# Seven block products for eight in the last batch's out-projection of an attention and feed-forward kernel

## The chip, the cores and the metric

One core of one Trainium2 chip. The time is the device time of one execution in microseconds (us), as a median over runs. A profile's times count from its own first instruction, and its span is some 1.7 us shorter than the device time. Two kernels are called faster or slower than each other from 2% on; a smaller difference can still be clear of noise, and then its interval says so.

## The reference

```python
def sm_attn(qq, kk, vv):
    s = scale * np.matmul(qq, kk.transpose(0, 1, 3, 2))
    ...                                   # row softmax -> a
    return np.matmul(a, vv)
p_packed = sm_attn(p, k, v)               # 8 batches, 8 heads, 32 packed rows, head size 64
out = sm_attn(q, p_packed, p_packed)      # 576 rows a head
x = out.transpose(0, 2, 1, 3).reshape(4608, 512)
h = x @ w_in                              # 512 -> 2048
g = h * np.cos(h)
return (g @ w_out).astype(np.float32)     # 2048 -> 512: the out-projection
```

## The kernel before

The eight batches run as a pipeline. While TensorE computes the hidden layer of batch b (`h_mm`, sixteen column blocks of 128), the out-projection of batch b-1 is fed in between as filler, one matmul per `fill` step.

```python
def recips(b):                     # for the NEXT batch, on VectorE
    ...
    V.reciprocal(r1[b], sums1[b])
    V.tensor_scalar(out=rs1[b], in0=r1[b], scalar1=scale, scalar2=None, op0=ALU.mult)   # 128x2

def normalise(b):                  # a2n: what h_mm(b) multiplies
    ...
    for y in range(2):
        V.scalar_tensor_tensor(out=a2n[b][:, y], in0=a2u[b][:, y], scalar=r1[b][:, y:y + 1],
                               in1=lns[b][:, y], op0=ALU.mult, op1=ALU.mult)   # two inputs in SBUF

def h_mm(b, fc):
    ...                            # 4 matmuls -> PSUM, cosine on ScalarE
    def rest():
        V.tensor_tensor(out=gT[b][:, fc, :]..., in0=ps[:, :, 0:HS], in1=csv, op=ALU.mult)  # PSUM and SBUF
        if fc % 8 == 7:
            G.tensor_copy(out=joint[b // 2][...], in_=gT[b][...])                # GpSimd

for s in range(3, B):
    ...
    permute_v(s + 1)               # GpSimd copy of the next batch's v
    ...
    recips(s + 1)
    ...
    sums2(s, 0); fill(5); sums2(s, 1)
    normalise(s)
    ...
    fill(13)
    slot(s, [(5, ...pp(s + 1)...), (10, ...pw2(s + 1)...)], 5, {10: 3})   # h_mm(s, 0..15), hooks, filler
set_filler(B - 1); fill(1000)      # last batch: 4 chunks x 16 matmuls of 128x512
tail_chunk(B - 1, 4)               # joint chunk of batches 6 and 7: 32 matmuls of 128x256
```

The softmax here doesn't subtract the row's maximum and nothing guards it: scores larger than these inputs give would overflow.

Of the kernel before, what the change touches and what calls it, by code (L numbers as in the profile page):

```python
# [8 lines left out]
FP32 = mybir.dt.float32  # L9
BF16 = mybir.dt.bfloat16  # L10
AF = mybir.ActivationFunctionType
ALU = mybir.AluOpType
# [3 lines left out]
def kernel(  # L16
# [8 lines left out]
    out: bass.AP,  # L25
):
    nc = tc.nc
    B, H, S, D = q.shape
    NP = p.shape[2]
    DM, DF = moe_w_in.shape  # L30
    scale = 1.0 / (D ** 0.5)
    NFC = DF // 128
    C = 6
    TP = S // C
    HS = S // 2
    PSUM = bass.MemoryType.PSUM
    EXP_SET = "natural_log_exp_and_others"
    SIN_SET = "trig_and_small"
# [1 line left out]
    const = ctx.enter_context(tc.tile_pool(name="const", bufs=1))  # L40
    bf_pool = ctx.enter_context(tc.tile_pool(name="bf", bufs=1))
    vp_pool = ctx.enter_context(tc.tile_pool(name="vp", bufs=2))
    att_pool = ctx.enter_context(tc.tile_pool(name="att", bufs=1))
    a2n_pool = ctx.enter_context(tc.tile_pool(name="a2n", bufs=2))
# [9 lines left out]
    ctx.enter_context(tc.manual_schedule())  # L54
    V, ACT, G = nc.vector, nc.scalar, nc.gpsimd

    w_in_bf = const.tile([128, 4, DF], BF16, name="w_in_bf")
    w_out_bf = const.tile([128, NFC, DM], BF16, name="w_out_bf")
    ident = const.tile([128, 128], BF16, name="ident")
    ones_blk = const.tile([128, 128], BF16, name="ones_blk")  # L60
# [12 lines left out]
    def copy(eng, out, in_):  # L73
        if eng is ACT:
            ACT.copy(out=out, in_=in_)  # L75
        else:
            eng.tensor_copy(out=out, in_=in_)  # L77
# [100 lines left out]
    def pp(b, own=False, engs=(V, ACT)):  # L178
        ps = bank() if own else psa()[:, 0, :]
        for hp in range(4):  # L180
            for j in range(C):
                c = 2 * (j % 3) + j // 3
                nc.tensor.matmul(ps[:, hp * 64:(hp + 1) * 64], vp[b][:, c, hp * 128:(hp + 1) * 128],  # L183
                                 a1T[b][0:TP, :, j, 32 * hp:32 * hp + 32], start=(j == 0), stop=(j == C - 1))
        pv = ps[:, 0:256].rearrange("p (a y x) -> p a y x", a=4, y=2)
        t = ppT[b % 2].rearrange("p (a y) x -> p a y x", y=2)
        for y in range(2):
            r = slice(64 * y, 64 * y + 64)
            copy(engs[0], t[r, :, y, :], pv[r, :, y, :])
        for y in range(2):  # L190
            r = slice(64 * y, 64 * y + 64)
            z = slice(64 - 64 * y, 128 - 64 * y)
            copy(engs[1], t[z, :, y, :], pv[r, :, y, :])
# [25 lines left out]
        evacuate()  # L219

    def s2(b):
        a2u[b] = att_pool.tile([128, 2, S], BF16, name="a2u", tag="a2u")
        ps = scores(ppT[b % 2], xT["q", b])
        for y in range(2):
            ACT.activation(out=a2u[b][:, y].rearrange("p (e x) -> p e x", e=2),  # L225
                           in_=ps[y][:, :, 0:HS], func=AF.Exp, scale=rs1[b][:, y:y + 1])

    def sums2(b, y):
        if b not in lns:
            lns[b] = att_pool.tile([128, 2, S], FP32, name="lns", tag="lns")  # L230
        ps = psa()
        for e in range(2):
            nc.tensor.matmul(ps[:, e, 0:HS], ones_blk, a2u[b][:, y, e * HS:(e + 1) * HS],  # L233
                             start=True, stop=True)
        ACT.activation(out=lns[b][:, y].rearrange("p (e x) -> p e x", e=2),  # L235
                       in_=ps[:, :, 0:HS], func=AF.Ln)

    def normalise(b):
        a2n[b] = a2n_pool.tile([128, 2, S], BF16, name="a2n", tag="a2n")
        for y in range(2):  # L240
            ACT.activation(out=lns[b][:, y], in_=lns[b][:, y], func=AF.Exp, scale=-1.0)  # L241
        for y in range(2):
            V.scalar_tensor_tensor(out=a2n[b][:, y], in0=a2u[b][:, y], scalar=r1[b][:, y:y + 1],  # L243
                                   in1=lns[b][:, y], op0=ALU.mult, op1=ALU.mult)

    gT, joint = {}, {}

    def h_mm(b, fc):
        if fc == 0:
            gT[b] = g_pool.tile([128, NFC, S], BF16, name="gT", tag="gT")  # L250
            if b % 2 == 0:
                joint[b // 2] = j_pool.tile([128, NFC, 128], BF16, name="joint", tag="joint")
        ps = psa()
        for y in range(2):
            for e in range(2):
                nc.tensor.matmul(ps[:, e, 0:HS], PPW[b][:, y, fc * 128:(fc + 1) * 128],  # L256
                                 a2n[b][:, y, e * HS:(e + 1) * HS], start=(y == 0), stop=(y == 1))
        cs = cos_pool.tile([128, S], BF16, name="cosT")
        csv = cs.rearrange("p (e x) -> p e x", e=2)
        ACT.activation(out=csv, in_=ps[:, :, 0:HS], func=AF.Sin, bias=PI_HALF)  # L260

        def rest():
            V.tensor_tensor(out=gT[b][:, fc, :].rearrange("p (e x) -> p e x", e=2),  # L263
                            in0=ps[:, :, 0:HS], in1=csv, op=ALU.mult)
            if fc % 8 == 7:
                j0 = (b % 2) * 64
                G.tensor_copy(out=joint[b // 2][:, fc - 7:fc + 1, j0:j0 + 64],  # L267
                              in_=gT[b][:, fc - 7:fc + 1, 512:576])
        return rest
# [1 line left out]
    n_out, out_eng = [0], [V, ACT]  # L271

    def pieces_of(b, c):
        ob = out[b * S:(b + 1) * S, :].rearrange("(p c) d -> c p d", c=C)
        if c == 4:
            o0 = out[(b - 1) * S:b * S, :].rearrange("(p c) d -> c p d", c=C)
            return [(0, 64, o0[5, 32:96]), (64, 128, ob[5, 32:96])]
        res, z = [], c * 128
        while z < c * 128 + 128:
            j, p0 = z // TP, z % TP  # L280
            n = min(TP - p0, c * 128 + 128 - z)
            res.append((z - c * 128, z - c * 128 + n, ob[2 * (j % 3) + j // 3, p0:p0 + n]))
            z += n
        return res
# [1 line left out]
    def n_chunks(b):  # L286
        return 5 if b % 2 and b < B - 1 else 4

    def tail_chunk(b, c):
        osb = o_pool.tile([128, DM], FP32, name="osb")  # L290
        for i in range(2):
            cols = slice(i * 256, i * 256 + 256)
            ps = O.tile([128, 256], FP32, name="ot", tag="ot")
            for fc in range(NFC):
                nc.tensor.matmul(ps, joint[b // 2][:, fc, :], w_out_bf[:, fc, cols],  # L295
                                 start=(fc == 0), stop=(fc == NFC - 1))
            copy((ACT, V)[i], osb[:, cols], ps)
            for (a, z, rows), q in zip(pieces_of(b, c), (nc.sync, nc.scalar)):
                q.dma_start(out=rows[:, cols], in_=osb[a:z, cols])

    def out_gen(b):
        groups = [(0, 1), (2,), (3,)] if b == 0 else [(c,) for c in range(n_chunks(b))]
# [18 lines left out]
    def set_filler(b):  # L321
        fill(1000)
        filler[0] = out_gen(b)
        filler[1] = 16 * n_chunks(b)
# [95 lines left out]
    def slot(s, hooks, keep=0, heavy={}):  # L420
        left = filler[1] - keep
        out_eng[:] = ACT,
        weight = [1 + heavy.get(fc, 0) for fc in range(NFC)]
        for fc in range(NFC):
            h_mm(s, fc)()
            quota = (left * sum(weight[:fc + 1])) // sum(weight) - (left + keep - filler[1])
            first = quota
            while hooks and hooks[0][0] == fc:
                if first == quota and fc in heavy:
                    first = quota // 2  # L430
                    fill(first)
                hooks.pop(0)[1]()
            fill(quota - first if first != quota else quota)

    def pw2(b, n=0, eng=None):
        ppw(b, n, eng)
        ppw(b, n + 1, eng)
# [69 lines left out]
    for s in range(3, B):  # L507
        nxt = s + 1 < B
        ACT.preload_act_table_set(EXP_SET)
        out_eng[:] = V,  # L510
        fill(1000)
        set_filler(s - 1)
        if nxt:
            permute_v(s + 1)
        s2(s)
        ppw(s, 2, V)
        if nxt:
            xbar("q", s + 1)
        fill(10)
        if nxt:  # L520
            s1(s + 1)
            ppw(s, 3, V)
            a1_xbar(s + 1)
            recips(s + 1)
            if s + 2 < B:
                xbar("k", s + 2)
                G.tensor_copy(out=gate, in_=xT["k", s + 2][0:1, 0, 0:1])  # L527
        else:
            ppw(s, 3, V)
        fill(4)  # L530
        sums2(s, 0)
        fill(5)
        sums2(s, 1)
        normalise(s)
        ACT.preload_act_table_set(SIN_SET)
        fill(13)
        for n, b in (("v", s + 2), ("q", s + 2), ("k", s + 3)):
            if b < B:
                load(n, b)
        slot(s, [(5, lambda: pp(s + 1, engs=(ACT, ACT))), (10, lambda: pw2(s + 1))] if nxt else [], 5, {10: 3})  # L540
    out_eng[:] = V, ACT
    set_filler(B - 1)
    fill(1000)
    tail_chunk(B - 1, 4)


# [28 lines left out]
```

## Time and profile before

| | before |
|---|---|
| median of the runs beside the change | 248.29 us (248.0 to 248.59) |
| profiled span | 246.8 us |
| TensorE busy | 94%, 78% of the chain that ended last |
| VectorE, ScalarE, GpSimd busy | 67%, 68%, 23% |
| last stage alone (from 224.95 us on) | 17.9 us of TensorE, then 4 us of copy and store |

Read it so: TensorE is at work nearly all the time, so its work is the time; other engines matter where they make TensorE wait. The chain is the work and the waits that ended last, followed back from the last instruction. The granted clock is the share of TensorE's full clock that the chip let it have. The profile's lines stand in the prediction below.

### The profile page before, as it was taken

To read this page: it belongs to the slowest core of one execution; us is meant where nothing else is said; L and a number is where in the kernel's file an instruction comes from. 1 tells how busy PE (TensorE), PEld (TensorE's weight loads), DVE (VectorE), ACT (ScalarE), POOL (GpSimd) and SP (SyncE) were. 2 spreads that over 40 slices of the span, in tenths; PEclk is the share of its full clock that TensorE was granted. 3 is DMA by queue.
4 is the path that set the end of the run, shared out by engine and by line. 5 is a ranking of instruction groups with operands and counts; after the bars stand their busy time and mean duration, and the time that the engine had idled before them with its cause. 6 is when DMAs were issued, how large, how long until landed. Compare 5 with 4: busy or idle time off the path is not lost.

```text
span 246.8 us, 5023 instructions
## 1 busy us (share of the span) xinstructions
PE 233.2 (94%) x1996; PEld 130.9 (53%) x2029; DVE 165.2 (67%) x248; ACT 169.0 (68%) x282; POOL 57.7 (23%) x70
## 2 busy tenths in 40 slices
PE   8788799999999999999999999999999999999993
PEld 3454374566545654565446554565456554665452
DVE  3549987677658776678767766678766684886110
ACT  2369799877576787888787776888778684873000
POOL 8342533240400355004503105030500100001000
PEclk9999999999999999999999999999999999999999
DMA  6999999999899999999999997999571113111133
GB/s 90 202 203 206 205 206 228 194 241 151 179 202 184 192 175 214 218 198 142 222 211 187 172 201 91 198 166 171 109 154 27 45 43 84 43 31 57 47 84 85
DMA packets 64231, 37.36 MB, mean 151 GB/s; under 512 B 36848, under 2 KB 59632, under 8 KB 64208
## 3 DMA queue, kind: packets, MB, share of 16 engines
q0 software_dynamic: 23152, 18.75, 50.0%
q1 hardware_dynamic: 40624, 18.09, 35.1%
q8 instruction: 16, 0.26, 0.4%
q10 hardware_dynamic: 432, 0.20, 0.4%
q14 instruction: 7, 0.06, 0.1%
HBM read 37.22 MB, written 9.44 MB: 189 GB/s over the span
## 4 chain that ended last, share of the span: by engine, by line
PE 78%; DMA 12%; issue 2%; DVE 2%; ACT 2%; POOL 2%; DVEq 0%; POOLq 0%
PE ot L309 46%; PE psA L256 21%; DMA vbf<-in_v_dram 10%; PE psA L207 3%; DMA a1T<-a 2%; PE psA L129 2%; PE psA L183 2%; DVE gT L263 2%; PE ot L295 1%; PE psA L233 1%; ACT cosT L260 1%; POOL vp L77 1%; ACT ppT L75 1%; POOL kbf L84 1%; PE ot L104 0%
## 5 line engine op out<-in xcount | busy, mean ns | idle before, releaser
L309 PE MATMUL ot<-w_out_bf,gT 128*128 128x512 bf16 x482 | 127.5, 379 | 2.0 <-issue 1.1
L263 DVE TENSOR_TENSOR gT<-psA,cosT 128x576 bf16<-128x576 f32 x128 | 93.8, 755 | 28.9 <-ACT cosT L260 28.2
L260 ACT ACTIVATE cosT<-psA 128x576 bf16<-128x576 f32 x128 | 82.4, 652 | 24.6 <-PE psA L256 22.1
L256 PE MATMUL psA<-a2n,PPW 128*128 128x288 bf16 x512 | 83.8, 286 | 1.6 <-DVE gT L263 0.4
L309 PEld LDWEIGHTS <-gT 128*128 128x128 bf16 x512 | 47.8, 98 | 43.4 <-issue 6.7
L256 PEld LDWEIGHTS <-PPW 128*128 128x128 bf16 x512 | 49.3, 98 | 34.6 <-issue 3.9
L77 DVE CAST PPW<-psA 128x1024 bf16<-128x1024 f32 (+1 forms) x23 | 26.9, 1175 | 11.6 <-PE psA L207 11.5
L267 POOL COPY joint<-gT 128x512 bf16<-128x512 bf16 x16 | 9.9, 616 | 82.5 <-DVE gT L263 82.5
L77 DVE COPY osb<-ot 128x512 f32<-128x512 f32 (+1 forms) x22 | 14.9, 678 | 17.5 <-PE ot L309 7.7
L77 POOL COPY vp<-vbf 96x3072 bf16<-96x3072 bf16 x7 | 19.3, 2751 | 6.3 <-DMA vbf<-in_v_dram 6.3
L75 ACT COPY osb<-ot 128x512 f32<-128x512 f32 (+1 forms) x15 | 8.5, 567 | 15.3 <-PE ot L309 10.6
L243 DVE SCALAR_TENSOR_TENSOR a2n<-a2u,r,lns 128x576 bf16<-128x576 bf16 x16 | 12.3, 812 | 7.3 <-ACT lns L241 7.3
L235 ACT ACTIVATE lns<-psA 128x576 f32<-128x576 f32 x16 | 10.1, 650 | 7.1 <-PE psA L233 6.5
L140 ACT ACTIVATE a<-psA 128x576 bf16<-128x576 f32 x16 | 10.3, 647 | 6.7 <-PE psA L129 6.7
L309 PE MATMUL ot<-w_out_bf,joint 128*128 128x512 bf16 x47 | 12.8, 379 | 0.1
L225 ACT ACTIVATE a2u<-psA,rs 128x576 bf16<-128x576 f32 x16 | 11.0, 737 | 1.4 <-PE psA L129 1.3
L75 ACT CAST ppT<-psA 64x128 bf16<-64x128 f32 x24 | 6.2, 260 | 7.0 <-DVE ppT L77 5.9
L207 PE MATMUL psA<-w_in_bf,ppT 64*32 64x512 bf16 x224 | 10.1, 380 | 0.0
L241 ACT ACTIVATE lns<-lns 128x576 f32<-128x576 f32 x16 | 10.0, 676 | 0.0
L347 PE MATMUL ot<-wz 128*128 128x512 bf16 x23 | 7.7, 468 | 1.4 <-DVE wz L358 1.2
L527 POOL COPY gate<-kT 1x1 bf16<-1x1 bf16 x3 | 0.5, 181 | 32.3 <-DMA kT<-kbf 32.3
L183 PEld LDWEIGHTS <-vp 96*128 96x128 bf16 x192 | 6.5, 98 | 2.3 <-issue 1.2
(73 smaller groups left out, 152.7 us busy)
## 6 DMA issues: line engine op xcount, KB each, us to landing
kbf<-in_k_dram POOLq DMA_DIRECT2D x8, 576.0 KB, 12.6
vbf<-in_v_dram POOLq DMA_DIRECT2D x8, 576.0 KB, 7.6
qbf<-in_q_dram POOLq DMA_DIRECT2D x8, 576.0 KB, 10.1
out_dram<-osb SPq DMA_DIRECT2D x24, 192.0 KB, 2.7
out_dram<-osb SPq DMA_DIRECT2D x22, 128.0 KB, 2.4
w_in_bf<-in_moe_w_in_dram POOLq DMA_DIRECT2D x4, 512.0 KB, 17.3
w_out_bf<-in_moe_w_out_dram POOLq DMA_DIRECT2D x4, 512.0 KB, 21.2
out_dram<-osb SPq DMA_DIRECT2D x26, 64.0 KB, 2.1
```

Source lines behind the costliest of these rows:

```text
L75: ACT.copy(out=out, in_=in_)
L77: eng.tensor_copy(out=out, in_=in_)
L140: ACT.activation(out=a1[b % 2][:, y, :, 0:TP].rearrange("p (e m) x -> p e m x", e=2), in_=ps[y][:, :, 0:HS].rearrange("p e (m x) -> p e m ...
L183: nc.tensor.matmul(ps[:, hp * 64:(hp + 1) * 64], vp[b][:, c, hp * 128:(hp + 1) * 128], a1T[b][0:TP, :, j, 32 * hp:32 * hp + 32], start=(j ...
L207: nc.tensor.matmul(ps[y][32 * x:32 * x + 32, :], ppT[b % 2][r, 2 * x + y, :], w_in_bf[r, x, n * 512:(n + 1) * 512], start=True, stop=True)
L225: ACT.activation(out=a2u[b][:, y].rearrange("p (e x) -> p e x", e=2), in_=ps[y][:, :, 0:HS], func=AF.Exp, scale=rs1[b][:, y:y + 1])
L235: ACT.activation(out=lns[b][:, y].rearrange("p (e x) -> p e x", e=2), in_=ps[:, :, 0:HS], func=AF.Ln)
L243: V.scalar_tensor_tensor(out=a2n[b][:, y], in0=a2u[b][:, y], scalar=r1[b][:, y:y + 1], in1=lns[b][:, y], op0=ALU.mult, op1=ALU.mult)
L256: nc.tensor.matmul(ps[:, e, 0:HS], PPW[b][:, y, fc * 128:(fc + 1) * 128], a2n[b][:, y, e * HS:(e + 1) * HS], start=(y == 0), stop=(y == 1))
L260: ACT.activation(out=csv, in_=ps[:, :, 0:HS], func=AF.Sin, bias=PI_HALF)
L263: V.tensor_tensor(out=gT[b][:, fc, :].rearrange("p (e x) -> p e x", e=2), in0=ps[:, :, 0:HS], in1=csv, op=ALU.mult)
L309: nc.tensor.matmul(pss[c], w, w_out_bf[:, fc, :], start=(fc == 0), stop=(fc == NFC - 1))
```

## The change

The last batch's four chunks of 128 rows are taken as two pairs. For each pair the product of a 256 x 2048 by a 2048 x 512 matrix is cut in 2 x 2 blocks, and seven block products with sums ahead of them and behind them replace eight. The sums of weight blocks (T, for both pairs) and of activation blocks (S, for each pair) must be made first, by engines other than TensorE; their buffers are those of inputs no longer needed (k, q, v for T, w_in for S).

```diff
+    def T_sums():
+        for n in ("k", "k", "q", "v"):
+            T.append(bf_pool.tile([128, 8, 256], BF16, name="T", tag=n + "bf", ...))
+        for out, in0, in1 in ((T[0], B_blk(0, 1), B_blk(0, 0)), (T[1], B_blk(1, 1), T[0]),
+                              (T[2], B_blk(1, 1), B_blk(0, 1)), (T[3], B_blk(1, 0), T[1])):
+            G.tensor_tensor(out=out, in0=in0, in1=in1, op=ALU.subtract)
+
+    def S_sums(b, p, eng, k0, k1): ...          # 4 sums on eng over row blocks k0 to k1
+    def last_out(b): ...                        # products, combining adds on VectorE, stores
...
             h_mm(s, fc)()
+            if s == B - 1 and fc in (3, 7):
+                for p in range(2):
+                    S_sums(s, p, G, fc // 2 - 1, fc // 2 + 1)
...
-        slot(s, [(5, ...pp...), (10, ...pw2...)] if nxt else [], 5, {10: 3})
-    out_eng[:] = V, ACT
-    set_filler(B - 1)
+        slot(s, [(5, ...pp...), ] + [(6, T_sums)] * (s == B - 2) + [(10, ...pw2...)] if nxt else [], 5, {10: 3})
     fill(1000)
-    tail_chunk(B - 1, 4)
+    for p in range(2):
+        S_sums(B - 1, p, V, 4, 8)
+    last_out(B - 1)
```

More of the change, by code (lines that the diff above doesn't have):

```diff
@@ L27 @@
     nc = tc.nc
-    B, H, S, D = q.shape
+    B, H, SQ, D = q.shape
     NP = p.shape[2]
@@ L33 @@
     C = 6
-    TP = S // C
-    HS = S // 2
+    TP = SQ // C
+    HS = SQ // 2
     PSUM = bass.MemoryType.PSUM
@@ L55 @@
     V, ACT, G = nc.vector, nc.scalar, nc.gpsimd
-    w_in_bf = const.tile([128, 4, DF], BF16, name="w_in_bf")
+    w_in_bf = const.tile([128, 4, DF], BF16, name="w_in_bf", tag="w_in_bf")
     w_out_bf = const.tile([128, NFC, DM], BF16, name="w_out_bf")
@@ L221, in s2 @@
     def s2(b):
-        a2u[b] = att_pool.tile([128, 2, S], BF16, name="a2u", tag="a2u")
+        a2u[b] = att_pool.tile([128, 2, SQ], BF16, name="a2u", tag="a2u")
         ps = scores(ppT[b % 2], xT["q", b])
@@ L229, in sums2 @@
         if b not in lns:
-            lns[b] = att_pool.tile([128, 2, S], FP32, name="lns", tag="lns")
+            lns[b] = att_pool.tile([128, 2, SQ], FP32, name="lns", tag="lns")
         ps = psa()
@@ L238, in normalise @@
     def normalise(b):
-        a2n[b] = a2n_pool.tile([128, 2, S], BF16, name="a2n", tag="a2n")
+        a2n[b] = a2n_pool.tile([128, 2, SQ], BF16, name="a2n", tag="a2n")
         for y in range(2):
@@ L249, in h_mm @@
         if fc == 0:
-            gT[b] = g_pool.tile([128, NFC, S], BF16, name="gT", tag="gT")
+            gT[b] = g_pool.tile([128, NFC, SQ], BF16, name="gT", tag="gT")
             if b % 2 == 0:
@@ L257, in h_mm @@
                                  a2n[b][:, y, e * HS:(e + 1) * HS], start=(y == 0), stop=(y == 1))
-        cs = cos_pool.tile([128, S], BF16, name="cosT")
+        cs = cos_pool.tile([128, SQ], BF16, name="cosT")
         csv = cs.rearrange("p (e x) -> p e x", e=2)
@@ L273, in pieces_of @@
     def pieces_of(b, c):
-        ob = out[b * S:(b + 1) * S, :].rearrange("(p c) d -> c p d", c=C)
+        ob = out[b * SQ:(b + 1) * SQ, :].rearrange("(p c) d -> c p d", c=C)
         if c == 4:
-            o0 = out[(b - 1) * S:b * S, :].rearrange("(p c) d -> c p d", c=C)
+            o0 = out[(b - 1) * SQ:b * SQ, :].rearrange("(p c) d -> c p d", c=C)
             return [(0, 64, o0[5, 32:96]), (64, 128, ob[5, 32:96])]
@@ L287, in n_chunks, with A_blk @@
         return 5 if b % 2 and b < B - 1 else 4
-    def tail_chunk(b, c):
-        osb = o_pool.tile([128, DM], FP32, name="osb")
-        for i in range(2):
-            cols = slice(i * 256, i * 256 + 256)
-            ps = O.tile([128, 256], FP32, name="ot", tag="ot")
-            for fc in range(NFC):
-                nc.tensor.matmul(ps, joint[b // 2][:, fc, :], w_out_bf[:, fc, cols],
-                                 start=(fc == 0), stop=(fc == NFC - 1))
-            copy((ACT, V)[i], osb[:, cols], ps)
-            for (a, z, rows), q in zip(pieces_of(b, c), (nc.sync, nc.scalar)):
-                q.dma_start(out=rows[:, cols], in_=osb[a:z, cols])
+    def A_blk(b, m, odd, k0, k1):
+        return gT[b][:, 2 * k0 + odd:2 * k1:2, m * 128:(m + 1) * 128]
@@ new lines, in B_blk @@
+    def B_blk(odd, n):
+        return w_out_bf[:, odd:NFC:2, n * 256:(n + 1) * 256]
+    T, S = [], {}
+    def T_sums():
+        for n in ("k", "k", "q", "v"):
+            T.append(bf_pool.tile([128, 8, 256], BF16, name="T", tag=n + "bf", bufs=2 if n == "k" else 1))
+        for out, in0, in1 in ((T[0], B_blk(0, 1), B_blk(0, 0)), (T[1], B_blk(1, 1), T[0]),
+                              (T[2], B_blk(1, 1), B_blk(0, 1)), (T[3], B_blk(1, 0), T[1])):
+            G.tensor_tensor(out=out, in0=in0, in1=in1, op=ALU.subtract)
@@ new lines, in S_sums @@
+    def S_sums(b, p, eng, k0, k1):
+        if not S:
+            t = const.tile([128, 2, 4, 8, 128], BF16, name="S", tag="w_in_bf")
+            S[0], S[1] = t[:, 0], t[:, 1]
+        A11, A12 = (A_blk(b, 2 * p, i, k0, k1) for i in range(2))
+        A21, A22 = (A_blk(b, 2 * p + 1, i, k0, k1) for i in range(2))
+        S1, S2, S3, S4 = (S[p][:, i, k0:k1, :] for i in range(4))
+        for out, in0, in1, op in ((S1, A21, A22, ALU.add), (S2, S1, A11, ALU.subtract),
+                                  (S3, A11, A21, ALU.subtract), (S4, A12, S2, ALU.subtract)):
+            eng.tensor_tensor(out=out, in0=in0, in1=in1, op=op)
@@ new lines, in last_out, with store, plus, then4 @@
+    def last_out(b):
+        pr = {}
+        def store(o, c, half=None, queues=(nc.sync, nc.sync, nc.sync)):
+            for (a, z, rows), q in zip(pieces_of(b, c), queues):
+                rows = rows.rearrange("p (a x) -> p a x", a=2)
+                h = slice(0, 2) if half is None else slice(half, half + 1)
+                q.dma_start(out=rows[:, h], in_=o[a:z, h])
+        def plus(out, in0, one):
+            if len(in0.shape) == 3:
+                in0, one = bass.broadcast_tensor_aps(in0, one.rearrange("p (a x) -> p a x", a=1))
+            V.tensor_tensor(out=out, in0=in0, in1=one, op=ALU.add)
+        for p in range(2):
+            S1, S2, S3, S4 = (S[p][:, i] for i in range(4))
+            m = {1: (A_blk(b, 2 * p, 0, 0, 8), B_blk(0, 0)), 2: (A_blk(b, 2 * p, 1, 0, 8), B_blk(1, 0)),
+                 3: (S4, B_blk(1, 1)), 4: (A_blk(b, 2 * p + 1, 1, 0, 8), T[3]),
+                 5: (S1, T[0]), 6: (S2, T[1]), 7: (S3, T[2])}
+            o1 = vp_pool.tile([128, 3, 256], FP32, name="o1", tag="vp")
+            o2 = o_pool.tile([128, 2, 256], FP32, name="osb", tag="osb")
+            u = att_pool.tile([128, 2, 256], FP32, name="u", tag=("lns", "a2u")[p])
+            def then4(ps, p=p, o1=o1, o2=o2, u=u):
+                plus(o2, ps, u[:, 1])
+                store(o2, 2 * p + 1)
+                plus(o1[:, 2], ps[:, 1], o1[:, 2])
+            def then3(ps, p=p, o1=o1):
+                plus(o1[:, 1], ps, o1[:, 2])
+                store(o1, 2 * p, 1, (nc.sync, nc.scalar, nc.sync))
+            def then2(ps, p=p, o1=o1, u=u):
+                plus(o1[:, 0:3:2, :], ps, u[:, 0])
+                store(o1, 2 * p, 0)
+            pr[p] = m, {1: lambda ps, u=u: ACT.copy(out=u[:, 0], in_=ps), 2: then2, 3: then3, 4: then4,
+                        7: lambda ps, u=u, o1=o1: plus(u[:, 1], ps, o1[:, 2])}
+        def products(names):
+            ps = O.tile([128, 2, 256], FP32, name="ot", tag="ot")
+            for i, (p, n) in enumerate(names):
+                lhs, rhs = pr[p][0][n]
+                for kp in range(8):
+                    nc.tensor.matmul(ps[:, i], lhs[:, kp, :], rhs[:, kp, :], start=kp == 0, stop=kp == 7)
+            if len(names) == 2 and names[0][0] == names[1][0]:
+                pr[names[0][0]][1][names[0][1]](ps)
+            else:
+                for i, (p, n) in enumerate(names):
+                    pr[p][1][n](ps[:, i])
+        products(((0, 1),))
+        ps = O.tile([128, DM], FP32, name="ot", tag="ot")
+        for fc in range(NFC):
+            nc.tensor.matmul(ps, joint[b // 2][:, fc, :], w_out_bf[:, fc, :], start=(fc == 0), stop=(fc == NFC - 1))
+        osb = o_pool.tile([128, DM], FP32, name="osb")
+        ACT.copy(out=osb, in_=ps)
+        for a, z, rows in pieces_of(b, 4):
+            nc.sync.dma_start(out=rows, in_=osb[a:z, :])
+        for names in (((0, 2), (0, 6)), ((0, 7),), ((0, 4), (0, 5)), ((0, 3), (1, 1)),
+                      ((1, 2), (1, 6)), ((1, 7),), ((1, 4), (1, 5)), ((1, 3),)):
+            products(names)
@@ L539 @@
                 load(n, b)
-        slot(s, [(5, lambda: pp(s + 1, engs=(ACT, ACT))), (10, lambda: pw2(s + 1))] if nxt else [], 5, {10: 3})
-    out_eng[:] = V, ACT
-    set_filler(B - 1)
+        slot(s, [(5, lambda: pp(s + 1, engs=(ACT, ACT))), ] + [(6, T_sums)] * (s == B - 2) + [(10, lambda: pw2(s + 1))] if nxt else [], 5, {10: 3})
     fill(1000)
-    tail_chunk(B - 1, 4)
+    for p in range(2):
+        S_sums(B - 1, p, V, 4, 8)
+    last_out(B - 1)
 _INS = ['q', 'k', 'v', 'p', 'moe_w_in', 'moe_w_out']
```

## The prediction

> **What bounds the kernel now.** I read the page first: busy time, then the chain that ended last.
>
> ```profile
> PE 233.2 (94%) x1996; PEld 130.9 (53%) x2029; DVE 165.2 (67%) x248; ACT 169.0 (68%) x282; POOL 57.7 (23%) x70
> PE 78%; DMA 12%; issue 2%; DVE 2%; ACT 2%; POOL 2%; DVEq 0%; POOLq 0%
> PE ot L309 46%; PE psA L256 21%; DMA vbf<-in_v_dram 10%; PE psA L207 3%; DMA a1T<-a 2%; PE psA L129 2%; PE psA L183 2%; DVE gT L263 2%; PE ot L295 1%; PE psA L233 1%; ACT cosT L260 1%; POOL vp L77 1%; ACT ppT L75 1%; POOL kbf L84 1%; PE ot L104 0%
> ```
>
> TensorE works 94% of 246.8 us and is 78% of the chain; the out-projection (L309) alone is 46%. So time taken off TensorE shortens the kernel, and a hole torn into it lengthens it by the hole. GpSimd is busy 23% and looks free.
>
> The change bites at the end, so next the chain's last entries (start, length, line), and the timeline of TensorE and of the end:
>
> ```profile
> 224.00 4.32 PE ot L309 x20
> 228.37 10.74 PE ot L309 x49
> 239.16 3.67 PE ot L295 x32
> ...
> 223.84 15.27 PE L309 MATMUL ot<-w_out_bf,gT 128*128 128x512 bf16 x69
> ...
> 242.91 0.42 DVE L77 COPY osb<-ot 128x256 f32<-128x256 f32 x1 [2.85 <-PE ot L295]
> ```
>
> From 223.84 on there is only the out-projection: 5 matmuls kept from batch 6, then 64 for the last batch's four chunks, then 32 narrow ones for the joint tail chunk. Pitch at 512 columns: 4.32/20 = 216 ns; over all 69, (239.16 - 223.84)/69 = 222 ns, so chunk changes cost a little. Pitch at 256 columns: (239.16 to 242.82, less some 0.16 for the last to drain)/32 = 109.5 ns. After the last matmul come a 0.42 us copy and 3.5 us of store until 246.8; that end stays much as it is.
>
> **What the Trainium skill says.** (1) "TensorE: Matmul & The Clock Gate", section "Wait — 56ns, not 53.3ns?": a warm stream costs N / 2.4 GHz + about 2.5 ns, so 215.8 ns for 512 columns and 109.2 for 256. The trace agrees (216; 109.5), with a weight load of 98 ns hidden under each. Thus halving the columns costs almost nothing, which is what seven for eight needs.
> (2) "VectorE: DVE Perf Modes", section "The perf-mode tier table": bf16 tensor_tensor in SBUF runs two elements a cycle, one with a PSUM input. L263 (576 columns, PSUM) at 755 ns fits the one; no two-input bf16 sum in SBUF is in this trace.
> (3) "GPSIMD Engine Reference", section "3.1 Elementwise — side-by-side cycle accounting": a two-input add of 2048 elements took 4497 ns there, about 2.6 cycles an element. This trace has only one-input copies: 2751 ns at 3072 columns, 616 at 512, so 0.83 ns a column plus 190.
> (4) "SBUF — State Buffer", section "Who interferes with whom": a VectorE instruction with two SBUF inputs and a GpSimd one that reads SBUF exclude each other; the second waits for the whole of the first. Nothing in this trace tests it: the sixteen two-input a2n products (L243) last 806 to 818 ns, none beside a GpSimd instruction.
>
> **The change, part by part.** *TensorE.* Before: 64 matmuls of 512 columns plus 32 of 256, 223.84 + 5 x 0.222 = 224.95 to 242.82, 17.9 us. After: two row pairs x 7 products x 8 = 112 matmuls of 256 columns, 112 x 109.3 = 12.24, plus the joint chunk now as 16 of 512, 16 x 215.8 = 3.45; with 0.16 of drain 15.85. That is 2.0 us less; with small costs at ten bank changes, as before at chunk changes, I take **1.7 us**.
>
> *The combining adds at the end* take PSUM and SBUF, so I price them as L77/L263: 512 columns 690 ns, 256 columns 424. Behind the last paired product stand 690 + 424 = 1.11 us of adds, while the last product takes TensorE 8 x 109.3 = 0.87. So the last add starts some 0.25 us late: **+0.25 us**. The earlier adds fit: a bank is wanted again one product later, which is at least 0.87 us, and no add run is longer than 1.11.
>
> *Weight sums T* (4 on GpSimd, 2048 columns): about 4.5 us each, 18 us. The listing of the built program puts them right behind the last value permutation, waiting for loads, the query transpose and each other; nothing holds them to column block 6 of the slot, where the source has them. The permutation and the VectorE stretch it then meets:
>
> ```profile
> 174.47 2.75 POOL L77 COPY vp<-vbf 96x3072 bf16<-96x3072 bf16 x1
> ...
> 178.54 0.15 DVE L151 RECIPROCAL r<-sums 128x2 f32<-128x2 f32 x1
> 178.73 0.17 DVE L152 TENSOR_SCALAR rs<-r 128x2 f32<-128x2 f32 x1
> 179.01 0.69 DVE L77 COPY osb<-ot 128x512 f32<-128x512 f32 x1
> 181.15 1.55 DVE L243 SCALAR_TENSOR_TENSOR a2n<-a2u,r,lns 128x576 bf16<-128x576 bf16 x2 [1.45 <-ACT lns L241]
> ...
> 182.50 0.65 PE L256 MATMUL psA<-a2n,PPW 128*128 128x288 bf16 x4
> ```
>
> T1 would run 177.2 to 181.7, T2 to 186.2, T3 to 190.7, T4 to 195.2. The two a2n products of batch 6 want 181.15 to 182.70, with two SBUF inputs each, and TensorE takes their result at 182.50 without slack. If nothing excludes, this costs 0. If T1 holds the first until 181.7, 0.6 us. If T2 slips between the two, another 4.5.
>
> *Row sums S.* Sixteen GpSimd sums of 256 columns, 190 + 256 x 2.1 = 0.73 us, a pitch of some 0.72. The last slot's VectorE times and the joint copy behind them:
>
> ```profile
> 214.31 1.46 DVE L263 TENSOR_TENSOR gT<-psA,cosT 128x576 bf16<-128x576 f32 x2 [0.16 <-ACT cosT L260]
> ...
> 224.02 1.47 DVE L263 TENSOR_TENSOR gT<-psA,cosT 128x576 bf16<-128x576 f32 x2 [0.16 <-ACT cosT L260]
> ...
> 225.55 0.62 POOL L267 COPY joint<-gT 128x512 bf16<-128x512 bf16 x1 [6.76 <-DVE gT L263]
> ```
>
> Block 3 is done at 215.1. From there 16 x 0.72 = 11.5 and two joint copies, 1.2: GpSimd is through at 227.8 instead of 226.2, since the second joint copy stands behind all sums in its queue. TensorE wants that copy for the ninth matmul of the joint chunk: 224.95 + 0.87 (first product) + 8 x 0.216 = 227.5. So **0.3 us** of wait, more if sums are slower or collide with VectorE's own eight sums. Those are 512 columns in two-element mode, (256 + 151)/0.96 = 0.42 us by the skill's formula, 3.4 us from 225.5, each with two SBUF inputs. Three turns of 0.42 taken by VectorE would bring the wait to 1.6. For TensorE itself VectorE's sums are in time: the second product begins at 229.3.
>
> Sum without exclusion: -1.7 + 0.25 + 0.3 = -1.15, so 247.3. With mild exclusion (0.6 at a2n, 1.3 more at the joint copy): 249.2.
>
> **The rivals.** *A: plain arithmetic, about 247.3.* For it: TensorE-bound end, pitch halves exactly, VectorE has 6 us idle gaps there. Against: it assumes GpSimd harmless.
> *B: the joint copy behind the sums is the new wait, 248 to 249.5.* For it: the queue order, which is certain; the sums' price is the skill's, not a measurement here. A pitch of 0.9 us alone would add 2.9.
> *C: the weight sums block the a2n products of batch 6, 252 to 253.* For it: the overlap in time and the page on SBUF. T2 waits for T1, which gives VectorE one chance to go first; the second product has to win again. Against: no trace here shows such a lock.
> *D: as C but twice.* The tiny scaling at 178.73 might be held too, pushing the output copy and both a2n products behind T2 and T3: 8 to 10 us, 256 to 258. It needs every turn lost.
> *E: VectorE slows in the last slot because GpSimd reads beside it.* L263 has one PSUM and one SBUF input, so by the page it is not concerned; I give it little.
>
> **Range and chances.** A gain above 2.0 us isn't there, so faster by 2% (under 243.5) is all but excluded: 0.01. I give A and B together 0.65, mild exclusion in both places 0.1, C 0.13, D 0.11; the kernel was tuned before, which speaks somewhat against a gross stall being left in. Only D, and C with B on top, pass 253.4: slower 0.14. The middle of this weight lies near **248.2 us**; the range that cuts a tenth at each end is 246.7 to 253.4.
>
> **What would show it right or wrong.** Right: product matmuls at a pitch of 109 to 110 ns; GpSimd sums of 2048 columns near 4.5 us starting at 177.2 and of 256 near 0.73; the second joint copy ending after 227; last add 0.2 to 0.3 us after TensorE's end. C or D: the a2n products of batch 6 start late or last several us, and TensorE stands idle near 182.7. Wrong altogether: product matmuls clearly slower than 110 ns (weight loads at 98 ns no longer hidden), VectorE's sums in one-element mode (0.69 us), or a time under 246, for which I see no source.

## The result, and the profile after

| | before | after |
|---|---|---|
| median, us | 248.29 | 256.86 (256.53 to 257.46) |
| ratio | | 1.0348, 95% interval 1.0322 to 1.0373 |
| profiled span, us | 246.8 | 255.7 |
| mean granted TensorE clock | 1.00 | 0.98 |
| TensorE busy 174 to 190 us | 15.73 of 16 | 9.25 of 16 |

The kernel became 8.6 us slower, and the time was lost long before the last stage, at the place where the weight sums run. The chain of the changed kernel, in the entries around 180 us (start, length, engine, tile and line):

```profile
178.71 2.40 issue
181.11 0.60 DVE osb L77
181.71 8.73 DVE a2n L243 x2
190.49 0.64 PE psA L256 x2
```

"issue" is time in which an engine waited for nothing that the profile shows: here the output copy (osb) stands behind something on VectorE. In the kernel before, this stretch of the chain was matmuls throughout. Now the end of the whole kernel hangs for nearly 9 us on two VectorE products. The timelines of GpSimd, VectorE and TensorE say why (start, length, instruction, and in brackets what ended idle time):

```profile
174.39 2.75 POOL L77 COPY vp<-vbf 96x3072 bf16<-96x3072 bf16 x1
177.10 4.07 POOL L302 TENSOR_TENSOR T<-w_out_bf 128x2048 bf16<-128x2048 bf16 x1
181.25 4.05 POOL L302 TENSOR_TENSOR T<-w_out_bf,T 128x2048 bf16<-128x2048 bf16 x1
185.26 4.56 POOL L302 TENSOR_TENSOR T<-w_out_bf 128x2048 bf16<-128x2048 bf16 x1
189.78 4.57 POOL L302 TENSOR_TENSOR T<-w_out_bf,T 128x2048 bf16<-128x2048 bf16 x1
...
178.65 2.55 DVE L152 TENSOR_SCALAR rs<-r 128x2 f32<-128x2 f32 x1
181.11 0.68 DVE L77 COPY osb<-ot 128x512 f32<-128x512 f32 x1
181.71 8.72 DVE L243 SCALAR_TENSOR_TENSOR a2n<-a2u,r,lns 128x576 bf16<-128x576 bf16 x2
...
185.97 0.66 PE L256 MATMUL psA<-a2n,PPW 128*128 128x288 bf16 x2 [3.38 <-DVE a2n L243]
190.49 0.64 PE L256 MATMUL psA<-a2n,PPW 128*128 128x288 bf16 x2 [3.85 <-DVE a2n L243]
```

The scaling of 256 numbers, 0.17 us before, lasts 2.55 us: it ends at 181.2, when the first weight sum ends at 181.17. That pushes the output copy and the first product past the start of the second sum. The two products, 1.55 us together before, last 8.72. The first ends about 185.9 (TensorE starts on it at 185.97), right after the second sum, and the third sum is 0.5 us longer than the two before it, as it waits in turn; the second product ends at 190.43, again just after a sum, and the fourth sum is longer too. TensorE stands idle 3.38 + 3.85 = 7.2 us.

The stage that was changed went as intended. TensorE's timeline at the end:

```profile
235.63 1.04 PE L359 MATMUL ot<-w_out_bf,gT 128*128 128x256 bf16 x8
236.50 3.62 PE L369 MATMUL ot<-w_out_bf,joint 128*128 128x512 bf16 x16
...
250.74 1.04 PE L359 MATMUL ot<-w_out_bf,S 128*128 128x256 bf16 x8
```

From 235.63 to 251.78 is 16.15 us without a hole, against 17.9 before.

### The profile page after: what moved, and what is told of

It reads as the page before. It is cut to its first block, busy times and chain, and to the rows that moved or that the text cites. A ratio compares the mean times of both kernels' runs of the same rounds, so it can differ in the third digit from the quotient of the medians.

```text
span 255.7 us, 5162 instructions
## 1 busy us (share of the span) xinstructions
PE 237.4 (93%) x2061; PEld 134.8 (53%) x2061; DVE 180.6 (71%) x262; ACT 169.5 (66%) x283; POOL 85.4 (33%) x90
## 4 chain that ended last, share of the span: by engine, by line
PE 73%; DMA 13%; DVE 7%; ACT 3%; issue 2%; POOL 0%; DVEq 0%; ACTq 0%; POOLq 0%
PE ot L386 38%; PE psA L256 20%; DMA qbf<-in_q_dram 7%; PE ot L359 5%; DVE a2n L243 3%; DMA vbf<-in_v_dram 3%; PE psA L207 3%; DMA a1T<-a 2%; PE psA L183 2%; PE psA L129 2%; ACT cosT L260 2%; DVE gT L263 2%; PE ot L369 1%; PE psA L233 1%; ACT ppT L75 1%
## 5 line engine op out<-in xcount | busy, mean ns | idle before, releaser
L386 PE MATMUL ot<-w_out_bf,gT 128*128 128x512 bf16 x448 | 120.9, 383 | 0.0
L263 DVE TENSOR_TENSOR gT<-psA,cosT 128x576 bf16<-128x576 f32 x128 | 93.9, 756 | 31.2 <-ACT cosT L260 30.5
L256 PE MATMUL psA<-a2n,PPW 128*128 128x288 bf16 x512 | 85.6, 290 | 8.5 <-DVE a2n L243 7.2
L386 PEld LDWEIGHTS <-gT 128*128 128x128 bf16 x448 | 41.9, 98 | 36.4 <-issue 6.8
L243 DVE SCALAR_TENSOR_TENSOR a2n<-a2u,r,lns 128x576 bf16<-128x576 bf16 x16 | 19.5, 1262 | 5.9 <-ACT lns L241 5.9
L140 ACT ACTIVATE a<-psA 128x576 bf16<-128x576 f32 x16 | 10.3, 647 | 6.7 <-PE psA L129 6.7
L77 DVE COPY osb<-ot 128x512 f32<-128x512 f32 x18 | 12.4, 689 | 2.0 <-PE ot L386 1.4
L313 POOL TENSOR_TENSOR S<-gT 128x256 bf16<-128x256 bf16 x8 | 5.3, 669 | 12.5 <-DVE gT L263 12.5
L302 POOL TENSOR_TENSOR T<-w_out_bf,T 128x2048 bf16<-128x2048 bf16 x2 | 8.6, 4312 | 0.1
```

Source lines behind the costliest of these rows:

```text
L77: eng.tensor_copy(out=out, in_=in_)
L140: ACT.activation(out=a1[b % 2][:, y, :, 0:TP].rearrange("p (e m) x -> p e m x", e=2), in_=ps[y][:, :, 0:HS].rearrange("p e (m x) -> p e m ...
L256: nc.tensor.matmul(ps[:, e, 0:HS], PPW[b][:, y, fc * 128:(fc + 1) * 128], a2n[b][:, y, e * HS:(e + 1) * HS], start=(y == 0), stop=(y == 1))
L263: V.tensor_tensor(out=gT[b][:, fc, :].rearrange("p (e x) -> p e x", e=2), in0=ps[:, :, 0:HS], in1=csv, op=ALU.mult)
L386: nc.tensor.matmul(pss[c], w, w_out_bf[:, fc, :], start=(fc == 0), stop=(fc == NFC - 1))
```

## The experiments

My theory after the result: GpSimd's weight sums, which start at 177.1 us, some 12 us before their place in the source (column block 6 of the slot, at 188.96 in the kernel before), keep VectorE's scaling and a2n products of batch 6 out; all else works. Rivals: the new products or the row sums cost what they should save; and the slow matmuls after the hole come from GpSimd reading the same weights, not from the clock.

### The weight sums after the a2n products

```diff
     def T_sums():
+        G.tensor_copy(out=gate, in_=a2n[B - 2][0:1, 1, 0:1])
         for n in ("k", "k", "q", "v"):
```

> One line more: a one-element GpSimd copy that reads the second a2n product of batch 6 stands ahead of the four weight sums, so they start at about 182.7 us and not 177.1. Main theory (the weight sums hold the two-input VectorE products of batch 6 back, and everything else of the change works as computed): the scaling takes 0.17 us again and the two a2n products 1.55, no hole in TensorE near 183, granted clock 1.00, and the gain of the last stage comes through: 248.3 - 1.4 = 246.9 us. Rival (the products or the sums of the last slot are what costs): still above 250.

Measured: 247.00 us (246.69 to 247.04, five runs) against 248.34, ratio 0.9941 (0.9928 to 0.9953), output right. The same two places in its timelines:

```profile
182.66 0.18 POOL L298 COPY gate<-a2n 1x1 bf16<-1x1 bf16 x1 [5.61 <-DVE a2n L243]
182.81 4.05 POOL L303 TENSOR_TENSOR T<-w_out_bf 128x2048 bf16<-128x2048 bf16 x1
...
178.56 0.17 DVE L152 TENSOR_SCALAR rs<-r 128x2 f32<-128x2 f32 x1
...
180.99 1.54 DVE L243 SCALAR_TENSOR_TENSOR a2n<-a2u,r,lns 128x576 bf16<-128x576 bf16 x2 [1.45 <-ACT lns L241]
```

The same sums, 5.7 us later, cost nothing, and the seven products save 1.34 us. This kernel beats both others; against the kernel before it is 0.6%, but the interval lies clear of 1. The rival that the products or row sums cost the time falls.

### The weight sums alone

```diff
 # the kernel before, tail unchanged
-        slot(s, [(5, ...pp...), (10, ...pw2...)] if nxt else [], ...
+        slot(s, [(5, ...pp...), ] + [(6, T_sums)] * (s == B - 2) + [(10, ...pw2...)] if nxt else [], ...
```

> The kernel before with only the four weight sums added in the place where the change has them (never used); no seven products, no row sums, output right. Main theory: the whole loss sits here and is some 10.3 us (7.7 of waiting for a2n and the rest from matmuls at a lower granted clock after the hole), so 258 to 259 us, slower than the change by the 1.4 us that the seven products save. Rival (the loss is in the last stage or in the row sums): near 248.3.

Measured: 258.76 us against 248.42, ratio 1.0403 (1.0364 to 1.0442). The four sums, whose results no matmul reads, cost 10.3 us; the two products last 8.73 us in its profile. So the loss is theirs, and the parts add up: 10.3 less the 1.3 that the products save is 9.0, against the 8.6 us of the change; the spread of these runs (258.04 to 259.44) is wider than what is left.

### Idle matmuls in the hole

```diff
         fill(13)
+        if s == B - 2:
+            warm(30)
```

> The change with 30 idle matmuls of 128x512 put into TensorE's queue ahead of the last-but-one slot, about 6.5 us of the hole of 7.2 filled, nothing else changed. If the matmuls after the hole run slowly because the clock was lowered in the hole (granted clock 0.76 from 190 to 202): the clock stays at 1.00, TensorE catches up about 2.5 us, 254 to 254.6. If those matmuls were slow for another reason (GpSimd reads the same weights): no gain, 256.9 or more.

Measured: 255.34 us, 1.5 less than the change, not the 2.5 expected. The a2n products still last 8.75 us. The granted clock from 190 to 202 us in both kernels, from the view of busy time by windows (the third figure from the end, before DMA share and GB/s), the change first:

```profile
190.00:202.00 12.00, 11.51 (x78) 6.79 (x78) 6.80 (x10) 6.75 (x14) 4.35 (x1) 0.76 0.10 23
```

```profile
190.00:202.00 12.00, 11.00 (x88) 7.15 (x90) 8.44 (x12) 8.19 (x16) 5.19 (x3) 1.00 0.16 41
```

So the lowered clock behind the hole is a consequence of the hole, and worth 1.5 us. GpSimd's reading of the same weights slows no matmul: from 191 to 194.6 us, beside the fourth sum, the 512-column matmuls here follow each other every 0.216 us, as in the kernel before, and in the change every 0.427. With this the loss against the kernel with the gate, 256.86 - 247.00 = 9.9 us, divides by my account into 7.9 (a2n ready at 190.43 and not 182.53), 1.5 for the clock, and 0.5 that I did not trace.

### The scaling on ScalarE

```diff
-        V.tensor_scalar(out=rs1[b], in0=r1[b], scalar1=scale, ...)
+        if b == B - 1:
+            ACT.mul(out=rs1[b], in_=r1[b], mul=scale)
+        else:
+            V.tensor_scalar(out=rs1[b], in0=r1[b], scalar1=scale, ...)
```

> Only the tiny scaling of the last batch's reciprocals goes to ScalarE; the weight sums start at 177.1 as in the change. If the scaling held at 178.65 is what made the first a2n product miss its turn before the second weight sum (scenario D of the prediction): the first product now starts near 181.2 and runs its 0.8 us, and only the second waits for the end of the second sum, some 4 us; a2n is ready about 186, TensorE's hole is near 3.5 us instead of 7.2, time 251 to 252.5. If the products wait in any case for two sums: no gain, 256 to 257.

Measured: 252.30 us (252.01 to 253.72), 4.6 less than the change. VectorE's timeline has the two products as

```profile
181.08 5.34 DVE L246 SCALAR_TENSOR_TENSOR a2n<-a2u,r,lns 128x576 bf16<-128x576 bf16 x2 [1.46 <-ACT lns L244]
```

and TensorE waits once, 3.63 us. So one small instruction made the first product miss its turn, which cost more than half of the loss.

### Memsets in place of the sums

```diff
-        for out, in0, in1 in ((T[0], ...), ...):
-            G.tensor_tensor(out=out, in0=in0, in1=in1, op=ALU.subtract)
+        for i in range(8):
+            G.memset(T[i % 4], 0.5)
```

> In place of the four weight sums eight GpSimd memsets of the same tiles (output wrong on purpose): GpSimd is busy from 177.1 on, writes SBUF but reads none. By the page SBUF - State Buffer a two-input VectorE instruction excludes only GpSimd instructions that read: the a2n products keep 1.55 us for both, and the time is near 246.9. The scaling, single-input, should still be stretched if it runs in a 2-port mode (it would need the shared write side too), up to one memset, some 1 to 2 us. If GpSimd activity as such holds VectorE back, the products stretch by up to one memset each.

Measured: 246.90 us, output wrong as intended. GpSimd is busy from 176.88 on, with a short gap at 180.43 where it waits for a transfer:

```profile
176.88 3.55 POOL L301 MEMSET T<- 128x2048 bf16 x2
180.60 10.54 POOL L301 MEMSET T<- 128x2048 bf16 x6 [0.18 <-DMA qT<-qbf]
...
178.45 2.00 DVE L152 TENSOR_SCALAR rs<-r 128x2 f32<-128x2 f32 x1
...
180.88 1.54 DVE L243 SCALAR_TENSOR_TENSOR a2n<-a2u,r,lns 128x576 bf16<-128x576 bf16 x2 [0.42 <-ACT lns L241]
```

The products run undisturbed beside the memsets, so neither GpSimd's being busy nor its writing keeps a two-input product out. What the memsets lack against the sums is reading SBUF. The last stage of the change has the case between, a GpSimd copy, which reads one input, beside one of VectorE's two-input row sums:

```profile
236.69 0.80 POOL L267 COPY joint<-gT 128x512 bf16<-128x512 bf16 x1
236.95 0.82 DVE L313 TENSOR_TENSOR S<-gT 128x512 bf16<-128x512 bf16 x1
```

The row sum took 0.82 us where it takes 0.41 alone, and ended after the copy. So GpSimd's reading is what keeps a two-input VectorE instruction out in these runs. In the memset run the scaling is stretched by writing alone, and it ended in the gap, not at the border of the first two memsets. The Trainium skill, "SBUF — State Buffer", section "Who interferes with whom", says that a scaling can run in a two-port mode, which contends with any GpSimd instruction; the 2.00 us fit, but that it ran in that mode no run shows.

### The sums in quarters: a wrong expectation

```diff
-            G.tensor_tensor(out=out, in0=in0, in1=in1, op=ALU.subtract)
+            for k0 in range(0, 8, 2):
+                G.tensor_tensor(out=out[:, k0:k0 + 2], in0=in0[:, k0:k0 + 2], in1=in1[:, k0:k0 + 2], op=ALU.subtract)
```

> Each weight sum in four GpSimd instructions of 512 columns (about 1.15 us by the line through 0.67 us at 256 and 4.05 at 2048), same start, same data, no gate. If a GpSimd instruction shuts VectorE's two-input instruction out for its own whole length, each of the three waits (scaling, first and second product) shrinks to at most 1.15 us: a2n ready 1.5 to 2.3 us late instead of 7.7, 248 to 249.5 us. If the two engines share bandwidth, or the total amount of GpSimd work counts: as slow as the change, 255 or more.

Measured: 263.22 us, the slowest of all. From its GpSimd and VectorE timelines:

```profile
190.26 4.47 POOL L303 TENSOR_TENSOR T<-w_out_bf,T 128x512 bf16<-128x512 bf16 x4
...
178.50 16.27 DVE L152 TENSOR_SCALAR rs<-r 128x2 f32<-128x2 f32 x1
```

Shorter instructions made it worse: the scaling waited from 178.50 to 194.77, until the last of the sixteen quarters had ended at 194.73. So "one waits for the other's one instruction" is not the whole of it. A stream of GpSimd instructions can shut VectorE out until it ends.

### Quarters, with the scaling on ScalarE

The edits of "The scaling on ScalarE" and of "The sums in quarters" together.

> Quarters as in the run with quarters, and the tiny scaling on ScalarE as in the run without it on VectorE; so only the two a2n products meet the sixteen quarter sums. In the run with quarters the scaling waited 16.27 us, through all sixteen, and the products never met one. Theory 1 (the scaling waits for a gap in GpSimd's stream, a two-input product only for the instruction in flight): each product waits at most one quarter, 1.1 us, the next quarter waits for the product; a2n ready 1 to 2 us late, 248 to 249.3 us. Theory 2 (GpSimd instructions that follow at once never hand over to anybody): the products wait until about 194.5 too, 260 to 263 us.

Measured: 262.13 us (260.88 to 263.18). VectorE's line:

```profile
180.96 13.85 DVE L246 SCALAR_TENSOR_TENSOR a2n<-a2u,r,lns 128x576 bf16<-128x576 bf16 x2 [1.46 <-ACT lns L244]
```

The longer product lasts 12.22 us. It is the first, and it ends at 193.18, 0.6 us after a quarter had ended at 192.57, among the last four. So theory 1's distinction falls: a two-input product can starve just as the scaling did.

### Quarters, so ordered that GpSimd pauses

```diff
+        for part in (jobs[:3], jobs[3:]):          # T1, T2, T4 depend on each other; T3 last
+            for k0 in range(0, 8, 2):
+                for out, in0, in1 in part:
+                    G.tensor_tensor(out=out[:, k0:k0 + 2], ...)
```

> Quarters again, scaling on VectorE again, but in an order in which two of three quarters need the one just before (first quarter of sums one, two and four, then the second quarters, and so on; the third sum last). GpSimd then has a gap of some 0.08 us ahead of each dependent quarter, as ahead of the second sum in the change. Theory 1: the scaling slips into the first such gap, waiting 1 to 2.3 us instead of 16.27; the products then wait for at most one quarter each; a2n ready 1 to 2.5 us late, 248 to 249.5 us. If the number of GpSimd instructions or the load as such kept the scaling out: 255 to 263 us, as with quarters in plain order.

Measured: 248.48 us against 248.57 of the kernel before; 14.7 less than the same sixteen instructions in plain order.

```profile
176.86 1.16 POOL L305 TENSOR_TENSOR T<-w_out_bf 128x512 bf16<-128x512 bf16 x1
178.10 2.39 POOL L305 TENSOR_TENSOR T<-w_out_bf,T 128x512 bf16<-128x512 bf16 x2
...
178.40 0.87 DVE L152 TENSOR_SCALAR rs<-r 128x2 f32<-128x2 f32 x1
...
180.83 3.01 DVE L243 SCALAR_TENSOR_TENSOR a2n<-a2u,r,lns 128x576 bf16<-128x576 bf16 x2 [0.96 <-ACT lns L241]
```

GpSimd pauses for 0.08 us ahead of each quarter that needs the one before: from 176.86 + 1.16 to 178.10, and again between the two quarters of the second line, at 179.25. The scaling started after the first pause and ends at 179.27, in the second. So a pause of 0.08 us is enough for VectorE to get its turn; both products, too, got in at such pauses, at 181.60 and 183.22.

### Is a pause needed?

Two more runs. In the first no sum reads another, so there is no pause ahead of the second (output wrong); in the second the sums are halves in plain order.

```diff
-(T[1], B_blk(1, 1), T[0]) ... (T[3], B_blk(1, 0), T[1])
+(T[1], B_blk(1, 1), B_blk(0, 0)) ... (T[3], B_blk(1, 0), B_blk(0, 1))
```

> Four weight sums of full length in the change's place, but none reads another (second and fourth sum take other blocks; output wrong on purpose). So GpSimd has no gap of 0.08 us ahead of the second sum. If it was that gap which let the scaling in at 181.2 in the change: the scaling now waits past the first sum, to the end of the second or further; time 257 to 263. If a long GpSimd instruction hands over at its end in any case (as the boundary of sums two and three suggests, where the first product got in): the scaling waits 2.5 us as in the change, 256 to 257.5.

```diff
+            for k0 in range(0, 8, 4):
+                G.tensor_tensor(out=out[:, k0:k0 + 4], in0=in0[:, k0:k0 + 4], in1=in1[:, k0:k0 + 4], ...)
```

> Each weight sum in two instructions of 1024 columns, plain order. If shutting out is a matter of following at once, whatever the length: as with quarters, the scaling waits to about 194, 260 to 264 us. If it depends on length (full length hands over at the end, quarters did not): between, the scaling passes at some boundary before 190, 253 to 259 us.

Measured: 261.43 and 261.40 us. The independent sums first, GpSimd's line and VectorE's:

```profile
176.82 16.08 POOL L302 TENSOR_TENSOR T<-w_out_bf 128x2048 bf16<-128x2048 bf16 x4
...
178.37 14.57 DVE L152 TENSOR_SCALAR rs<-r 128x2 f32<-128x2 f32 x1
```

The halves, VectorE's lines:

```profile
178.69 0.61 DVE L152 TENSOR_SCALAR rs<-r 128x2 f32<-128x2 f32 x1
...
181.12 14.03 DVE L243 SCALAR_TENSOR_TENSOR a2n<-a2u,r,lns 128x576 bf16<-128x576 bf16 x2 [1.22 <-ACT lns L241]
```

Without the pause the scaling waits through all four long sums, which end at 192.90; with it, in the change, it waited for one. So in the change the dependence of the second sum on the first is what kept the loss at 9 and not at 13 us. (The run also freed the fourth sum from the second; ahead of that one the change shows no pause.) But the halves refuse a simple rule, and neither branch of their expectation fits. There the scaling did get in, at 179.3, between two halves that do not depend on each other, and then the products starved. In the change itself the products got in ahead of the third and the fourth sum, which follow without a visible pause. So in these runs, wherever GpSimd paused while VectorE waited, VectorE got in; who wins where GpSimd's next instruction follows at once is left open.

## Why the prediction was wrong

- **Time and range: wrong.** 256.86 us lies above the range to 253.4. The step that failed is VectorE's wait for the weight sums: the sum of the prediction counts it as 0 ("If nothing excludes, this costs 0"), the mild case as 0.6 us, and "I give A and B together 0.65" rests on that. The runs showed in its place that the weight sums hold the scaling (2.55 us and not 0.17) and both products (8.72 and not 1.55), so that a2n was ready at 190.43 and not at 182.70, and TensorE stood idle for 7.2 us. The weight sums alone cost 10.3 us, the lowered clock included.
- **Rival D, at 0.11, is what happened,** in its mechanism too: the scaling at 178.7 was held first, then the copy and both products were pushed behind T2 and T3. That its 256 to 258 us also hit the time is partly luck: it left out the clock (1.5 us) and the gain of the last stage (1.15 by the prediction's sum), which nearly cancel, and it took 4.5 us for a sum that lasted 4.05.
- **Why so little weight for it.** The start of T1 (177.2 predicted, 177.10 measured), the overlap and the page that names the exclusion all spoke for a wait. Against it stood only that no trace had tested the lock, and that "the kernel was tuned before, which speaks somewhat against a gross stall being left in". Two lines of the trace before could have been read the other way:

```profile
66.56 0.67 DVE L152 TENSOR_SCALAR rs<-r 128x2 f32<-128x2 f32 x1
...
77.97 0.18 POOL L499 COPY gate<-a2n 1x1 bf16<-1x1 bf16 x1 [9.61 <-DVE a2n L243]
```

The scaling, 0.17 us in seven of its eight places, took 0.67 in the one beside which GpSimd was issuing DMAs: a hint, not a proof, that GpSimd can hold it. And ahead of batch 3's copy of v the kernel before already has a gate that makes GpSimd wait for a2n, in the same form as the line that the first experiment added. Why it was put there is not on record; but a kernel that was tuned with such a guard speaks for a stall, not against one, where new GpSimd work comes in unguarded. (One reading is loose: two a2n products of the trace before do stand beside a GpSimd entry, a DMA issue at 20.01, and kept their 0.81 us.)

- **"It needs every turn lost": too hopeful.** The turns are not lost one by one: the scaling's loss caused the first product's (with the scaling on ScalarE the kernel is 4.6 us faster), as D's own description has it. And D was not the worst that could happen: plain quarters were 6 us worse still.
- **TensorE's 1.7 us: right.** 17.9 to 16.15 us, and the product matmuls follow each other every 109 ns.
- **The late last add, 0.25 us: about right.** It ended 0.71 us after TensorE's last matmul, against 0.51 before, so 0.20 later.
- **0.3 us of wait for the joint copy: not there.** GpSimd's sums of 256 columns took 0.67 us and followed each other 0.66 apart on the mean ((230.06 - 225.43) / 7), not 0.72; the joint copy ended at 237.49, and the ninth joint matmul was due at 236.50 + 8 x 0.216 = 238.2. Rival B falls. The collision of VectorE's own row sums with GpSimd's is real but small: two of the eight took 0.78 and 0.82 us, the others the 0.41 to 0.42 that were predicted.
- **Rival E: rightly dismissed.** L263 averaged 756 ns after, 755 before.
- **Not foreseen:** the hole also lowered the clock, 1.5 us. The Trainium skill has it in "TensorE: Matmul & The Clock Gate", section "Why this matters for your kernels" (no idle gaps above some 3 us); two gaps of 3.38 and 3.85 us and a granted clock of 0.76 behind them agree.

The gated kernel is the case without exclusion: 247.0 us, against the prediction's sum of 247.3 for it. The 0.3 us between are as much as the wait for the joint copy that did not come.

## What to carry to other kernels

An engine that looks idle is not free: before work is given to GpSimd, look where its queue will really start it (at its last wait, not at its place in the source) and which VectorE instructions with two SBUF inputs, or small scalings in SBUF, fall beside it. If one of those is on the critical path, make the GpSimd work wait for it: a one-element copy as gate turned a loss of 8.6 us into a gain of 1.3. Cutting the GpSimd work into smaller pieces was no remedy here without pauses between them: quarters and halves in plain order cost 4.5 to 6.4 us more than the whole sums.

## What the Trainium skill lacked or had wrong

- "SBUF — State Buffer", section "Who interferes with whom": that a two-input VectorE instruction is kept out by GpSimd instructions that read and not by those that write agrees (8.72 us beside sums, 1.54 beside memsets).
- The same page, section "Summary: rules for kernel authors": that the second of the two "fully blocks until the first finishes" is too mild. A VectorE instruction waited through a whole run of GpSimd instructions, 16.27 us to the end of sixteen quarters (each about 1.16), 14.57 to the end of four long sums.
- The page has nothing on pauses: 0.08 us between dependent GpSimd instructions let VectorE in, at 181.2 in the change and at 179.27 in the chained run. What decides without a pause, neither the page nor these runs tell.
- "GPSIMD Engine Reference", section "3.1 Elementwise — side-by-side cycle accounting": it has 4497 ns for 2048 fp32 elements of a two-input add and no figure for bf16. Here a bf16 subtraction of 2048 took 4.05 us undisturbed, and a bf16 sum of 256 took 0.67, so 1.89 ns an element.
